# Strassen's algorithm for six of eight column pairs of a second matrix product, and what is moved to make room for it

## The chip, the cores and the metric

The kernel runs on one core of a Trainium2 chip. The time is device microseconds (us) of one execution. Three executions of the kernel before took 1072.84, 1072.2 and 1070.15 us; the median is 1072.2 us. TensorE (PE in the profile) multiplies matrices and writes to PSUM, a memory of eight banks of 512 f32 columns. VectorE (DVE), ScalarE (ACT) and GpSimd (POOL) do the elementwise work, and SyncE (SP) only issues transfers (DMA).

## The reference

Eight batches, eight heads of dimension 64 (512 columns in all), 576 tokens, 32 landmarks, 2048 hidden columns.

```python
def _attn_ref(q, k, v):            # per batch and head
    q_lm, k_lm = mean of q, k over 18 neighbouring tokens      # 32 landmarks
    A, Bm, C = softmax(q k_lm'), softmax(q_lm k_lm'), softmax(q_lm k')
    Z = Bm.T / (norm1(Bm) * norminf(Bm) + 1e-06)
    for _ in range(6):
        Z = 2 * Z - Z @ Bm @ Z
    return A @ Z @ C @ v

def _moe_ref(x, w_ch1, w_ch2):
    mixed = real(fft(fft(x, axis=1), axis=2))
    u = x + mixed
    un = (u - mean(u)) / sqrt(var(u) + 1e-06)
    return u + relu(un @ w_ch1) @ w_ch2
```

## The kernel before

**Numbers.** Products that must be exact to f32 are made of f16 halves: a value is split into `hi` and `lo`, and `mm3` issues three matmuls, hi·hi, hi·lo and lo·hi. The weights come as 64-bit floats, which VectorE rebuilds to f32 by bit operations (`weights`, in 32 pieces of 512 columns: 16 of the first matrix, 16 of the second). Only when all pieces of a matrix are there is its largest magnitude known, hence its scale `wsc`, and only then are its pieces split into halves (`halve`).

**Attention** runs batch by batch in generators. `tokens` loads q, k and v, makes the landmark means `lm`, the scores of all tokens and their softmax, transposes the softmax on TensorE (`AT`), and makes the Fourier sums `CS`. `landmarks` makes the 32 by 32 matrix `Bm`, C and C·v, runs six steps of the pseudo-inverse with E (128x128, block diagonal) against `RE` (32 columns of the power of E and 64 columns of the product with C·v), and then the small matrices `Wt`, `Wx` and `WC`. `mix` turns all of it into the rows `u` in tiles of 128 tokens (4.5 tiles a batch, 36 in all; it makes two tiles of u, normalises both in `norm`, splits them and has SP transpose them by DMA into `unT`).

**Feed-forward** (`mlp`) takes two tiles at a time: 18 chunks of 256 tokens. In a chunk, pair i (of eight) of the hidden blocks is made by `first` matmuls: 24 of 128x256 into a bank `h`. ScalarE applies relu and makes the high half, VectorE makes the low half. `second` multiplies pair i into two banks `acc` (one for each tile), 12 matmuls of 128x512. It comes LAG = 2 pairs behind the first product. After pair 7, VectorE adds `acc` to u, and SP writes it out.

**Order.** A small planner with its own clock (`run`) emits the program: attention first, weights second, feed-forward last. A generator yields until its inputs should be there by the planner's estimates (`till`, with MARGIN = 1.5 us on top), and whoever is ready is emitted. TensorE runs exactly in this order; for the other engines the compiler's scheduler sets the order. So feed-forward matmuls stand between the steps of attention. PSUM is given out as four banks `at` for attention, two for `h` and two for `acc`.

Nearly every VectorE, ScalarE and GpSimd instruction has the line of one helper (L121), and every matmul L197 (a transpose on TensorE L202), so groups are told apart by the names of their tiles.

Of the kernel before, what the change touches and what calls it, by code (L numbers as in the profile page):

```python
# [17 lines left out]
P = 128  # L18
# [8 lines left out]
BIG, MID, ROW, UB, HB, NT, PSH = 8, 7, 6, 7, 4, 3, 2  # L27
# [98 lines left out]
class Kernel:  # L126
    def __init__(self, ctx, tc, NB, q, k, v, w1, w2, t1, t1t, t2, diag, mask, out):
# [6 lines left out]
        self.ps_at, self.ps_h, self.ps_o = psum("ps_at", 8 - PSH - TCH), psum("ps_h", PSH), psum("ps_o", 1)  # L134
        self.loads = {}
        self.now, self.there, self.read, self.used = 0.0, {}, {}, []
# [10 lines left out]
        self.whole = [self.cp.tile([P, NF + 1, 512], F32, name=f"w{w}") for w in range(2)]  # L147
# [22 lines left out]
    def psum(self):  # L170
        t = self.ps_at.tile([P, 512], F32, name="at")
        self.used.append(t.name)
        return t
# [14 lines left out]
    def till(self, *aps, banks=0, more=0.0):  # L188

        last = len(self.used) + banks - (8 - PSH - TCH)  # L190
        free = [self.read.get(n, 0.0) for n in self.used[max(0, last - banks) : max(0, last)]]
        return max(0.0, max([0.0] + free + [self.there.get(a.name, 0.0) for a in aps]) + (MARGIN + more if len(self.unT) > 3 else M0) - self.now)
# [40 lines left out]
    def weights(self):  # L233
        nc = self.nc
        V, A = self.V, self.A
        whole = self.whole
        slots = [[t[:, i] for i in range(NF + 1)] for t in whole]
        am = [self.cp.tile([P, NF], F32, name=f"wmax{w}") for w in range(2)]
        hl = [[t.bitcast(F16).rearrange("p (y m) -> p y m", y=2) for t in ss] for ss in slots]
        self.w1s = [t.rearrange("p y (c f) -> p y c f", c=KT) for t in hl[0]]  # L240
        self.w2s = hl[1]
# [18 lines left out]
        def scale(w):  # L260
            a2 = self.small(1, "wm2")
            V.tensor_reduce(a2, am[w], AX.X, ALU.max)
            yield self.till(a2)
            e, r = yield from self.pow2(a2, 1, f"wp{w}")
            es.append(e)
            V.tensor_scalar(sc[:, w : w + 1], r[:, 0:1], (2.0**6, 2.0**14)[w], None, ALU.mult)

        def halve():
            w, f = pieces[sum(self.split_w)]
            self.split(hl[w][f][:, 0], hl[w][f][:, 1], slots[w][f + 1], sc[:, w : w + 1])  # L270
            self.split_w[w] = f + 1

        for i, (w, f) in enumerate(pieces):
            while len(mags) < min(2 * NF, i + 1 + PREP):
                j = len(mags)
                while len(self.wraw) < min(2 * NF, j + 1 + AHEAD):
                    self.raw()
                if self.raw_there[j] > self.now:
# [4 lines left out]
                prepare(j)  # L283
            rv = self.wraw[i].rearrange("p (m x) -> p m x", x=2)
            top, low = rv[:, :, 1], rv[:, :, 0]
            x, dst = mags[i].bitcast(I32), slots[w][f + 1]
# [11 lines left out]
            if es:  # L298
                halve()
# [14 lines left out]
    def raw(self):  # L314


        i = len(self.wraw)
        w, f = divmod(i, NF)
        room = self.whole[1].rearrange("p i m -> p (i m)").bitcast(I32)
        if w == 0:  # L320
            raw = room[:, 1024 * (f % 8) + 512 : 1024 * (f % 8) + 1536]
            src = self.w1.bitcast(I32).rearrange("(c p) f -> p c f", p=P)
            self.nc.sync.dma_start(raw.rearrange("p (c f) -> p c f", c=KT), src[:, :, 256 * f : 256 * f + 256])
        else:
            at = {3: 9, 4: 11, 5: 13, 6: 15, 11: 13, 12: 15}.get(f)
            if at:
                raw = room[:, 512 * at : 512 * at + 1024]
            else:
                raw = self.big().bitcast(I32)[:, 0:1024]
# [6 lines left out]
    def load(self, b):  # L336
# [3 lines left out]
        res = []  # L340
        for g in range(2):
            kf, qf = self.big(), self.big()
            gs = slice(2 * g, 2 * g + 2)
            nc.sync.dma_start(kf[:, 0 : 2 * S].rearrange("p (r t) -> p r t", r=2), self.k[b, :, gs])
            nc.sync.dma_start(qf[:, 0 : 16 * SEG].rearrange("p (r t) -> p r t", r=2), self.q[b, :, gs])
            for t in (kf, qf):
                self.there[t.name] = self.arrival(0.59)
            res.append([kf, qf])
        for g in range(2):
            for i in range(EARLY if b == 0 else 0):  # L350
                self.raw()
            vf = self.big()
            nc.sync.dma_start(vf.rearrange("p (c d) -> p c d", c=5), self.v[b, g].rearrange("(c p) d -> p c d", p=P))
            self.there[vf.name] = self.arrival(0.66)
            res[g].append(vf)
        self.loads[b] = res

    def tokens(self, b, st):
# [9 lines left out]
        qhs = []  # L368
        for g in range(2):
# [7 lines left out]
            qhs.append(self.big().bitcast(F16))  # L377
            A.activation(qhs[g][:, 0:NQ], qf, AF.Abs, accum_out=am[:, g : g + 1])
# [24 lines left out]
        qm = [h[:, 0:2048].rearrange("p (y r t) -> p y r t", y=2, r=2) for h in qhs]  # L403
        qr = [h[:, 2048:2304].rearrange("p (y r t) -> p y r t", y=2, r=2) for h in qhs]
        for g in range(2):
            qs = loads[g][1][:, 0:NQ].rearrange("p (x t) -> p x t", t=2 * SEG)
# [7 lines left out]
        while b == 1 and self.seconds < NF // 2 - HB:  # L414
            yield 0.5
# [5 lines left out]
        for u in range(3):  # L421
            yield self.till(qhs[min(u, 1)])
# [22 lines left out]
        for u in range(3):  # L445
            ae, w = aes[u], 512 if u < 2 else 128
            yield self.till(ae, banks=1)
            AT = (self.mid() if u < 2 else self.row()).bitcast(F16)[:, 0 : 2 * w].rearrange("p (y t) -> p y t", y=2)
            ps = self.psum()
            for j in range(w // 128):  # L450
                tr(ps[:, 128 * j : 128 * j + 128], ae[:, 128 * j : 128 * j + 128], self.ident)
            split(AT[:, 0], AT[:, 1], ps[:, 0:w], 1.0)
# [11 lines left out]
            else:  # L464
                F2 = ae
            Fh = (self.mid() if u < 2 else self.row()).bitcast(F16)[:, 0 : 2 * w].rearrange("p (y t) -> p y t", y=2)
            A.copy(Fh[:, 0], F2)
            self.G.tensor_tensor(Fh[:, 1], F2, Fh[:, 0], ALU.subtract)
            Fs.append(Fh)
        CS = self.big().bitcast(F16).rearrange("p (g y x t) -> p g y x t", g=2, y=2, x=2)  # L470
# [20 lines left out]

    def landmarks(self, b, st):
# [4 lines left out]
        m4g = lambda m: self.mask4.unsqueeze(1).unsqueeze(3).broadcast_to([P, 2, 4, m])  # L497
        wide = lambda src, m: src.unsqueeze(2).broadcast_to([P, 2, 4, m])
        Bd = sm.tile([P, 2, 32], F32, name="Bd")
        RE = sm.tile([P, 2, 96], F32, name="RE", bufs=3)  # L500
# [25 lines left out]
        while b == 1 and self.seconds < NF // 2 - HB:  # L526
            yield 0.5

        for g in range(2):
            kv = loads[g][0][:, 0 : 2 * S].rearrange("p (r t) -> p r t", r=2)  # L530
# [23 lines left out]
        yield self.till(nrm)  # L554

        psn = self.psum()
        mm(psn[:, 0:128], self.ones_bd.rearrange("p a b -> p (a b)"), nrm.rearrange("p g x m -> p (g x m)"))
        cm = self.small(4, "cm")
        V.tensor_reduce(cm, psn[:, 0:128].rearrange("p (x m) -> p x m", m=32), AX.X, ALU.max)
        ci = self.small(2, "ci")  # L560
        cmv = cm.rearrange("p (g x) -> p g x", x=2)
        V.tensor_tensor(ci, cmv[:, :, 0], cmv[:, :, 1], ALU.mult)
        V.tensor_scalar(ci, ci, 1e-6, None, ALU.add)
        V.reciprocal(ci, ci)
        nci = self.small(2, "nci")
        V.tensor_scalar(nci, ci, -1.0, None, ALU.mult)
        Bbd = sm.tile([P, 2, 4, 32], F32, name="Bbd", bufs=1)
        V.tensor_tensor(Bbd, wide(nrm[:, :, 0, :], 32), m4g(32), ALU.mult)
# [381 lines left out]
```

## Time and profile before

| | |
|---|---|
| median of three runs | 1072.2 us |
| the profiled execution | 1069.82 us, span 1068.0 us (1.8 us lie outside the span) |
| TensorE busy | 983.9 us, 92% of the span |
| VectorE, ScalarE, GpSimd busy | 615.7, 351.6, 111.5 us |
| TensorE idle after 300 us | under 6 us |
| mean granted TensorE clock | 0.973 |

In the groups, "idle before" is what the engine stood still just ahead of an instruction. "mean ns of one" of a matmul holds its pipeline; the spacing of matmuls is read from the chain of waits, where a run such as "x24" is given with its length. A granted clock of 1.00 is full speed. The lines themselves stand in the prediction.

### The profile page before, as it was taken

How to read it: one execution, taken by the hardware profiler on the slowest of the kernel's cores; microseconds unless marked ns; L12 is line 12 of the kernel's file. 1: busy time of each engine (PE TensorE's matmuls, PEld its weight loads, DVE VectorE, ACT ScalarE, POOL GpSimd, SP SyncE). 2: the span in 40 equal slices, each digit the busy share in tenths (PEclk: the TensorE clock that was granted, in tenths of full speed). 3: DMA queues.
4: the chain of work that ended last, by engine and by line, in shares of the span. 5: the costliest groups of instructions: out<-in, count | busy, mean ns of one | idle time of the engine just before them, and what ended most of it. 6: DMA issues, size and time to landing. Idle time of an engine off the chain costs nothing.

```text
span 1068.0 us, 19629 instructions
## 1 busy us (share of the span) xinstructions
PE 983.9 (92%) x8062; PEld 684.6 (64%) x8062; DVE 615.7 (58%) x1673; ACT 351.6 (33%) x797; POOL 111.5 (10%) x125
## 2 busy tenths in 40 slices
PE   1554778999999999999999999999999999999998
PEld 0433535667776676666777677677766677766665
DVE  7889888768562566446745674567451654341111
ACT  4566755334231333123322332233311332111110
POOL 0101102021011020110202020202010020110000
PEclk9766989999999999999999999999999999999999
DMA  9824402223011130110402040114011000110000
GB/s 327 310 99 118 135 25 91 70 50 136 24 39 22 51 109 21 20 41 11 159 1 58 3 153 8 45 17 143 27 41 20 21 1 21 21 48 15 9 20 20
DMA packets 71018, 68.16 MB, mean 64 GB/s; under 512 B 41360, under 2 KB 59792, under 8 KB 70800
## 3 DMA queue, kind: packets, MB, share of 16 engines
q1 hardware_dynamic: 70928, 66.91, 20.3%
q8 instruction: 63, 1.03, 0.4%
q14 instruction: 27, 0.22, 0.1%
HBM read 48.02 MB, written 9.44 MB: 54 GB/s over the span
## 4 chain that ended last, share of the span: by engine, by line
PE 86%; DVE 8%; issue 2%; ACT 2%; DMA 1%; POOL 0%; SPq 0%; ACTq 0%; DVEq 0%
PE acc L197 34%; PE h L197 34%; PE at L197 16%; DVE w L121 2%; PE at L202 2%; DVE row L121 2%; DVE mid L121 1%; ACT row L121 1%; DVE lm L121 1%; DMA big<-q_dram 0%; ACT mid L121 0%; DVE asum L121 0%; DVE big L121 0%; DVE u L121 0%; DVE RE L121 0%
## 5 line engine op out<-in xcount | busy, mean ns | idle before, releaser
L197 PE MATMUL h<-unT,w 128*128 128x256 f16 x3456 | 414.0, 274 | 19.9 <-DMA unT<-row 10.4
L197 PE MATMUL acc<-w,h 128*128 128x512 f16 x1680 | 395.2, 380 | 0.0
L197 PEld LDWEIGHTS <-w 128*128 128x128 f16 x3456 | 335.9, 98 | 92.2 <-issue 19.0
L197 PEld LDWEIGHTS <-h 128*128 128x128 f16 x1680 | 161.7, 98 | 160.9 <-issue 4.1
L121 DVE SCALAR_TENSOR_TENSOR h<-h 128x512 f16<-128x512 f32 x140 | 96.4, 688 | 246.6 <-ACT h L121 246.1
L121 ACT ACTIVATE h<-h 128x512 f16<-128x512 f32 x140 | 83.4, 596 | 359.5 <-PE h L197 359.0
L121 POOL TENSOR_TENSOR r<-ve,mhalf 128x2 f32<-128x2 f32 (+1 forms) x20 | 13.7, 683 | 445.9 <-DVE ve L121 445.9
L197 PEld LDWEIGHTS <-mid 128*128 128x128 f16 x432 | 39.8, 103 | 17.8 <-issue 7.4
L121 POOL TENSOR_TENSOR row<-row 128x512 f16<-128x512 f32 (+1 forms) x44 | 46.6, 1073 | 44.1 <-ACT row L121 44.1
L197 PEld LDWEIGHTS <-big 128*128 128x128 f16 (+1 forms) x768 | 40.6, 104 | 13.0 <-issue 2.4
L121 DVE SCALAR_TENSOR_TENSOR row<-at,scw,row 128x262 f32<-128x262 f32 (+1 forms) x48 | 21.4, 486 | 44.2 <-ACT row L121 31.5
L121 ACT CAST row<-row 128x512 f16<-128x512 f32 (+1 forms) x44 | 23.5, 559 | 70.7 <-DVE row L121 69.9
L121 DVE TENSOR_REDUCE lm<-big 128x32 f32<-128x576 f32 (+1 forms) x48 | 43.8, 943 | 2.7 <-DMA big<-k_dram 2.3
L121 POOL TENSOR_TENSOR mid<-mid,asum 128x512 f32<-128x512 f32 x14 | 14.8, 1055 | 291.7 <-DVE asum L121 291.7
L121 ACT ACTIVATE row<-w 128x512 f32<-128x512 f32 x54 | 33.8, 640 | 21.9 <-DVE w L121 11.4
L121 DVE SCALAR_TENSOR_TENSOR u<-at,scw,row 128x128 f32<-128x128 f32 (+3 forms) x120 | 38.9, 388 | 0.0
L121 POOL TENSOR_TENSOR mid<-mid 128x256 f32<-128x256 f32 (+1 forms) x32 | 31.6, 993 | 65.9 <-DVE mid L121 53.6
L197 PE MATMUL at<-RE,E 128*128 128x96 f32 (+1 forms) x192 | 30.1, 282 | 9.0 <-DVE RE L121 9.0
L197 PEld LDWEIGHTS at<-RE,E 128*128 128x128 f32 x192 | 27.9, 200 | 15.1 <-DVE RE L121 6.6
L197 PE MATMUL at<-mid,big 128*128 128x262 f16 (+1 forms) x288 | 34.1, 290 | 0.0
L121 DVE SCALAR_TENSOR_TENSOR u<-acc,wsc,u 128x512 f32<-128x512 f32 x36 | 26.8, 746 | 12.0 <-PE acc L197 11.7
L121 ACT ACTIVATE w<-w,wsc 128x512 f16<-128x512 f32 x32 | 23.0, 718 | 18.4 <-DVE w L121 12.9
(165 smaller groups left out, 968.5 us busy)
## 6 DMA issues: line engine op xcount, KB each, us to landing
w<-w_dram SPq DMA_DIRECT2D x22, 512.0 KB, 8.8
big<-v_dram SPq DMA_DIRECT2D x16, 640.0 KB, 8.5
big<-q_dram SPq DMA_DIRECT2D x16, 584.0 KB, 5.4
big<-k_dram SPq DMA_DIRECT2D x16, 576.0 KB, 4.3
out_dram<-u SPq DMA_DIRECT2D x36, 256.0 KB, 2.0
big<-w_dram SPq DMA_DIRECT2D x10, 512.0 KB, 7.9
unT<-row SPq DMA_TRANSPOSE x72, 2.4
t<-t_dram SPq DMA_DIRECT2D x1, 1048.0 KB, 10.0
```

The source lines that it names most:

```text
L121: return call(out, *args, **kw)
L197: self.nc.tensor.matmul(out, a, b, start=start, stop=stop, skip_group_check=True)
L202: self.nc.tensor.transpose(out, a, ident)
```

## The change

It has five parts.

1. **Second product.** For pairs 0 to 5 the 2x2 blocks (two tiles of 128 tokens by two hidden blocks, times two hidden blocks by two halves of 256 output columns) are multiplied by Strassen's algorithm in the form with seven products: 7 x 3 matmuls of 128x256 instead of 12 of 128x512. Pairs 6 and 7 stay as they were. The seven sums live in four banks, and after pair 7 they are put together by two ScalarE copies and eight VectorE instructions.
2. **Its left operand.** After relu (ScalarE, to f32 `hf`), VectorE makes four sums or differences of 128 columns, ScalarE makes the high halves of all seven blocks (896 columns), GpSimd the low halves. There is one `hf` buffer until the weights are split, then two; three buffers `h`.
3. **Its right operand.** `halve2` scales the pair (ScalarE, 1024 columns), VectorE makes four differences of 256 columns, ScalarE the high halves (256 and three times 512), VectorE the low halves of 256 and 512, GpSimd those of 512 twice. The raw pieces of the weights now go through a ring of five places, and the first chunk holds at most three pairs `h` before `second` has to begin.
4. **Attention.** It keeps two banks as soon as the second product has begun. The pseudo-inverse is a generator of its own (`inverse`), which carries 64 columns instead of 96, ends in one more product G of 128 columns, and runs beside C·v. The softmax of batches 2 to 7 is transposed by DMA (six more DMA transposes a batch) instead of nine TensorE transposes. v is loaded later, into five instead of eight `big` buffers, and v of batch 0 lies where the last first-matrix weights will lie.
5. **Start of a batch.** A batch may begin as soon as the batch ahead has its `WC`, not its last `mix`.

```diff
-BIG, MID, ROW, UB, HB, NT, PSH = 8, 7, 6, 7, 4, 3, 2
+BIG, MID, ROW, UB, HB, NT, PSH, PSO = 5, 7, 6, 6, 3, 2, 2, 4
+NS = 6
+W2AT = 3 * NS + 4
...
-        self.ps_at, self.ps_h, self.ps_o = psum("ps_at", 8 - PSH - TCH), psum("ps_h", PSH), psum("ps_o", 1)
+        self.ps_at, self.ps_h, self.ps_o = psum("ps_at", 8 - PSH - PSO), psum("ps_h", PSH), psum("ps_o", 1)
...
+        def halve2():
...
+                A.activation(src, src, AF.Copy, scale=sc[:, 1:2])
+                B11, B12, B21, B22 = (src[:, 256 * x : 256 * x + 256] for x in range(4))
+                T13, T24 = self.row(512), self.row(512)
+                (T1, T3), (T2, T4) = ((r[:, 0:256], r[:, 256:512]) for r in (T13, T24))
+                for out, a, b in ((T1, B12, B11), (T3, B22, B12), (T2, B22, T1), (T4, B21, T2)):
+                    V.tensor_tensor(out, a, b, ALU.subtract)
+                flat = t.rearrange("p y x d -> p y (x d)")
+                for a, b, x, eng in ((0, 256, B11, V), (256, 768, src[:, 512:1024], V), (768, 1280, T13, self.G), (1280, 1792, T24, self.G)):
+                    A.copy(flat[:, 0, a:b], x)
+                    eng.tensor_tensor(flat[:, 1, a:b], x, flat[:, 0, a:b], ALU.subtract)
...
+            if b >= 2:
+                for y in range(2):
+                    nc.sync.dma_start_transpose(AT[:, y].rearrange("p (c t) -> p c t", t=P), hl[:, y])
...
+    def inverse(self, st, nrm, nci):
...
+        for it in range(6):
+            yield self.till(E, EP, banks=1, more=NM)
+            c0, c1 = (0 if it < 5 else 32), (64 if it > 0 else 32)
+            ps = self.psum()
+            for g in range(2):
+                mm(ps[:, 64 * g + c0 : 64 * g + c1], flat(E, g), EP[:, g, c0:c1])
...
+        for g in range(2):
+            mm(ps[:, 128 * g : 128 * g + 128], flat(Pbd, g), flat(Bbd, g))
...
+        seven = ((0, 0, 4), (2, 1, 0), (6, 2, 1), (3, 6, 2), (4, 3, 7), (5, 5, 5), (1, 4, 6))
...
-            for t in range(TCH):
-                for x in range(2):
-                    f = 2 * i + x
-                    mm3(acc[t], lambda y: h[:, y, x, P * t : P * t + P], lambda y: self.w2s[f][:, y, :],
-                        start=(f == 0), stop=(f == NF - 1))
+            if i < NS:
+                hv = h.rearrange("p (y x t) -> p y x t", y=2, x=7)
+                for a, b, o in seven:
+                    mm3(acc[o // 2][:, 256 * (o % 2) : 256 * (o % 2) + 256], lambda y: hv[:, y, a], lambda y: self.w2s[i][:, y, b],
+                        start=(i == 0 and o in (0, 2, 4, 7)), stop=(i == NF // 2 - 1))
                     yield 0.0
...
+            if i == NF // 2 - 1:
+                us = self.utiles[TCH * ch : TCH * ch + 2]
...
+                V.tensor_tensor(us[0], us[0], r0, ALU.add)
+                V.tensor_tensor(us[1], us[1], r1, ALU.add)
...
+                while len(late) >= HB:
+                    yield from second(*late.pop(0))
+                h = self.wk.tile([P, 14 * P], F16, name="h", bufs=HB)
+                if i < NS:
+                    f = self.hf[i % 2 if self.split_w[1] == NF else 0]
+                    A11, A21, A12, A22, S1, S2, S4 = (f[:, x] for x in range(7))
+                    A.activation(f[:, 0:4].rearrange("p x t -> p (x t)"), ps, AF.Relu)
+                    V.tensor_tensor(S1, A21, A22, ALU.add)
+                    V.tensor_tensor(A21, A11, A21, ALU.subtract)
+                    V.tensor_tensor(S2, S1, A11, ALU.subtract)
+                    V.tensor_tensor(S4, A12, S2, ALU.subtract)
+                    f, hv = f.rearrange("p x t -> p (x t)"), [h[:, 896 * y : 896 * y + 896] for y in range(2)]
+                    A.copy(hv[0], f)
+                    self.G.tensor_tensor(hv[1], f, hv[0], ALU.subtract)
```

Where instructions now stand shows in three places. The first is VectorE once the second weight matrix has its scale: `wsc` is the scale, `w_74` the second matrix, `row` work space, `Bd` and `bs` belong to batch 1's attention. Before:

```order
L121 RECIPROCAL wp_r<-wp_e 128x1
L121 TENSOR_SCALAR wsc<-wp_e 128x1
L121 TENSOR_SCALAR wsc<-wp_r 128x1
L121 TENSOR_SCALAR Bd<-at 128x64
L121 TENSOR_REDUCE bmx<-Bd 128x2
L121 TENSOR_TENSOR Bd<-Bd,bmx 128x64
L121 SCALAR_TENSOR_TENSOR w_74<-w_74,wsc 128x512
L121 TENSOR_REDUCE bs<-Bd 128x2
```

After, on the same engine at the same place:

```order
L125 TENSOR_SCALAR wsc<-wp_r 128x1
L125 TENSOR_TENSOR row<-w_74 128x256 x2
L125 TENSOR_TENSOR row<-w_74,row 128x256
L125 TENSOR_TENSOR row<-w_74 128x256
L125 TENSOR_TENSOR row<-w_74,row 128x256
L125 TENSOR_TENSOR w_74<-w_74 128x256
L125 TENSOR_TENSOR w_74<-w_74 128x512
L125 TENSOR_TENSOR row<-w_74 128x256
```

One split of 512 columns for each block, with attention between, has become six instructions for each pair, most of them with both inputs in SBUF, and batch 1's attention stands behind the first pairs.

The second place is GpSimd in the same stretch: `r` belongs to the normalisation of batch 0, `mid` and `asum` to batch 1's softmax. Before:

```order
L121 TENSOR_TENSOR r_923<-ve,mhalf 128x2
L121 TENSOR_TENSOR row<-row 128x512 x2
L121 TENSOR_TENSOR mid<-mid,asum 128x512 x2
L121 TENSOR_TENSOR row<-row,asum 128x128
L121 TENSOR_TENSOR mid<-mid 128x256
```

After:

```order
L125 TENSOR_TENSOR r_926<-ve,mhalf 128x2
L125 TENSOR_TENSOR row<-row 128x512 x2
L125 TENSOR_TENSOR h<-hf,h 128x896 x3
L125 TENSOR_TENSOR w_74<-row,w_74 128x512 x7
L125 TENSOR_TENSOR h<-hf,h 128x896
L125 TENSOR_TENSOR w_74<-row,w_74 128x512 x3
L125 TENSOR_TENSOR h<-hf,h 128x896
L125 TENSOR_TENSOR w_74<-row,w_74 128x512
L125 TENSOR_TENSOR h<-hf,h 128x896
L125 TENSOR_TENSOR w_74<-row,w_74 128x512
L125 TENSOR_TENSOR mid<-mid,asum 128x512 x2
```

Where GpSimd had nothing to do between batch 0 and batch 1, six low halves of `h` and twelve of the weights now stand.

The third place is TensorE at the beginning of chunk 6, whose second tile is the first of batch 3 (`Wx` against `mid` is the last matmul of that tile in `mix`). Before, the last such matmul lies three pairs back, and the chunk follows on ordinary pairs:

```order
L197 MATMUL acc_4768<-w_74,h 128x512
L197 LDWEIGHTS h
L197 MATMUL acc_4769<-w_74,h 128x512
L197 LDWEIGHTS w_73
L197 MATMUL h<-unT,w_73 128x256
```

After, the whole way from that matmul to the first of chunk 6, with repeated rows left out:

```order
L209 MATMUL at<-Wx,mid 128x8x32
...
L209 MATMUL acc_5216<-w_74,h 128x256
...
L209 MATMUL acc_5215<-w_74,h 128x512
...
L209 MATMUL at<-mid,big 128x262
...
L209 MATMUL acc_5215<-w_74,h 128x512
L209 MATMUL at<-lm,qbd 64x32 x4
L209 LDWEIGHTS w_73
L209 MATMUL h<-unT,w_73 128x256
```

Between the two stand 21 matmuls of 128x256 and 12 of 128x512 of the second product, 12 of 128x262 of `mix`, and the first four of batch 4. The same sequence, without the last four, stands ahead of chunk 15 (the first tiles of batch 7).

More of the change, by code (lines that the diff above doesn't have):

```diff
@@ L170, in psum @@
     def psum(self):
-        t = self.ps_at.tile([P, 512], F32, name="at")
+        if not self.second_begun and len(self.used) % (8 - PSH) >= 8 - PSH - PSO:
+            t = self.ps_o.tile([P, 512], F32, name=f"acc{len(self.used) % (8 - PSH) - (8 - PSH - PSO)}")
+        else:
+            t = self.ps_at.tile([P, 512], F32, name="at")
+            self.used_at.append(t.name)
         self.used.append(t.name)
@@ L188, in till @@
     def till(self, *aps, banks=0, more=0.0):
-        last = len(self.used) + banks - (8 - PSH - TCH)
-        free = [self.read.get(n, 0.0) for n in self.used[max(0, last - banks) : max(0, last)]]
+        used, n = (self.used_at, 8 - PSH - PSO) if self.second_begun else (self.used, 8 - PSH)
+        last = len(used) + banks - n
+        free = [self.read.get(n, 0.0) for n in used[max(0, last - banks) : max(0, last)]]
         return max(0.0, max([0.0] + free + [self.there.get(a.name, 0.0) for a in aps]) + (MARGIN + more if len(self.unT) > 3 else M0) - self.now)
@@ L283, in weights @@
                 prepare(j)
+            while i >= 10 and not self.v0_used:
+                yield 0.3
             rv = self.wraw[i].rearrange("p (m x) -> p m x", x=2)
             top, low = rv[:, :, 1], rv[:, :, 0]
-            x, dst = mags[i].bitcast(I32), slots[w][f + 1]
+            x, dst = mags[i].bitcast(I32), f32[w][f]
             V.tensor_scalar(x, x, 3, None, ALU.logical_shift_left)
@@ L351, in load @@
                 self.raw()
[L352 to L356, printed above, removed]
+            self.nc.sync.dma_start(tiles[g].rearrange("p (c d) -> p c d", c=5), self.v[b, g].rearrange("(c p) d -> p c d", p=P))
+            self.there[tiles[g].name] = self.arrival(0.66)
+        return tiles
     def tokens(self, b, st):
@@ L413, in tokens @@
                 yield self.till(qhs[0], kbd)
-        while b == 1 and self.seconds < NF // 2 - HB:
+        st["split"] = True
+        while b == 1 and self.seconds < NF // 2 - 4:
             yield 0.5
@@ L469, in tokens @@
             Fs.append(Fh)
+        while "v" not in st:
+            yield 0.3
         CS = self.big().bitcast(F16).rearrange("p (g y x t) -> p g y x t", g=2, y=2, x=2)
@@ L553, in landmarks @@
             crs.append(cr)
[L554 to L568, printed above, removed]
-        yield self.till(Bbd, Ces[0])
-        pst = self.psum()
-        for g in range(2):
-            tr(pst[:, 128 * g : 128 * g + 128], Bbd[:, g].rearrange("p a b -> p (a b)"), self.ident)
-        BT = sm.tile([P, 2, P], F32, name="BT", bufs=1)
-        A.copy(BT.rearrange("p g m -> p (g m)"), pst[:, 0:256])
+        if b > 0:
+            while "split" not in st:
+                yield 0.3
+            vs = self.load_v(b, [self.big(), self.big()])
+        else:
+            vs = self.v0
+        st["v"] = True
+        yield self.till(Ces[0])
         ETs = []
@@ L656, in landmarks @@
             for x in range(2):
+                yield self.till(banks=1)
                 ps = self.psum()
@@ L851, in attention @@
         for b in range(self.NB):
-            while self.folded < b - 1 or (b > 0 and sum(self.split_w) < NF):
+            while self.w_done < b - 1 or (b > 0 and sum(self.split_w) < NF):
                 yield 0.5
```

279 lines of the change are left out of this document (181 added, 98 removed).

## Prediction

> **What bounds the kernel now.** I read the page first: the busy line, the slices, the chain.
>
> ```profile
> PE 983.9 (92%) x8062; PEld 684.6 (64%) x8062; DVE 615.7 (58%) x1673; ACT 351.6 (33%) x797; POOL 111.5 (10%) x125
> PE   1554778999999999999999999999999999999998
> DVE  7889888768562566446745674567451654341111
> PE 86%; DVE 8%; issue 2%; ACT 2%; DMA 1%; POOL 0%; SPq 0%; ACTq 0%; DVEq 0%
> ```
>
> TensorE is full from the ninth slice on (27 us each); its 84 us of idle time lie in the first 200 us, where VectorE is the busy one. So matmuls count from there on, and before it what VectorE must do. Next the chain's end and the windows, which price both:
>
> ```profile
> 1040.86 2.59 PE acc L197 x12
> 1043.45 2.62 PE h L197 x24
> ...
> 120.00:140.00 20.00, 13.35 (x99) 9.75 (x99) 19.93 (x35) 15.33 (x34) 0.00 (x0) 0.93 0.34 110
> 140.00:160.00 20.00, 14.80 (x76) 7.36 (x75) 17.02 (x50) 9.29 (x16) 0.00 (x0) 0.90 0.00 1
> 160.00:180.00 20.00, 17.31 (x220) 10.74 (x219) 17.79 (x54) 12.16 (x30) 3.67 (x5) 1.00 0.37 120
> 180.00:200.00 20.00, 18.90 (x149) 13.05 (x148) 15.99 (x39) 6.22 (x15) 3.27 (x4) 1.00 0.22 64
> 700.00:800.00 100.00, 100.00 (x874) 71.26 (x873) 61.31 (x178) 30.48 (x74) 11.59 (x13) 1.00 0.18 57
> ```
>
> A 128x256 matmul costs 2.62 / 24 = 0.109 us, a 128x512 one 2.59 / 12 = 0.216: half the columns is half the time, although each has its weight load. In 120 to 140 us VectorE is busy 19.93 of 20: it rebuilds the weights, and TensorE waits.
>
> **The gain on TensorE.** A Strassen pair costs 21 x 0.109 = 2.29 us instead of 2.59. With 18 chunks of six pairs that is 108 x 0.30 = 32.1 us less. The attention's matmuls:
>
> ```profile
> 172.24 0.61 PE L197 MATMUL at<-BT 128*128 128x128 f32 x4
> 172.68 0.71 PE L202 MATMUL at<-ident,mid 128*128 128x128 f32 x5
> 173.23 0.81 PE L197 MATMUL acc<-w,h 128*128 128x512 f16 x3
> ```
>
> Five transposes take 173.23 - 172.68 = 0.55 us, so nine in each of six batches are 54 x 0.11 = 5.9 less. G is four passes like those of BT (172.68 - 172.24 = 0.44) in eight batches, 3.5 more. Steps with 64 instead of 96 columns I count as equal: they wait for VectorE more than they compute. Gain: 32.1 + 5.9 - 3.5 = 34.5 us.
>
> **The head: the second matrix is prepared later.** The scale of the second matrix is there at 145.6 us, and splits follow at once:
>
> ```profile
> 139.77 0.16 DVE L121 TENSOR_REDUCE wm<-wmax 128x1 f32<-128x16 f32 x1
> 145.46 0.15 DVE L121 TENSOR_SCALAR wsc<-wp_r 128x1 f32<-128x1 f32 x1
> 146.40 0.75 DVE L121 SCALAR_TENSOR_TENSOR w<-w,wsc 128x512 f16<-128x512 f32 x1
> 46.52 0.69 DVE L121 TENSOR_TENSOR mid<-mid,asum 128x512 f32<-128x512 f32 x1
> 47.12 0.28 DVE L121 TENSOR_TENSOR row<-row,asum 128x128 f32<-128x128 f32 x1
> 47.92 0.75 DVE L121 TENSOR_TENSOR mid<-mid 128x256 f32<-128x256 f32 x2
> 267.40 0.42 POOL L121 TENSOR_TENSOR row<-row 128x128 f16<-128x128 f32 x1
> 268.17 1.16 POOL L121 TENSOR_TENSOR mid<-mid 128x512 f16<-128x512 f32 x1 [0.34 <-ACT mid L121]
> L121 ACT CAST row<-row 128x512 f16<-128x512 f32 x36 | 21.1, 617 | 70.7 <-DVE row L121 69.9 <-POOL row L121 0.6
> L121 ACT ACTIVATE big<-big,sc 128x1024 f16<-128x1024 f32 x16 | 18.4, 1148 | 0.0
> L121 DVE SCALAR_TENSOR_TENSOR big<-big,sc 128x1024 f16<-128x1024 f32 x16 | 20.5, 1279 | 1.0 <-ACT big L121 1.0
> ```
>
> From here on the first chunk's pairs 3 to 5 and the six Strassen weight pairs are made together, since only three buffers `h` may wait. Until the sixth weight pair is there, this must run:
> - VectorE with two SBUF inputs: 30 of 128x256 at 0.38 = 11.3; six of 512 at 0.69 = 4.1; twelve of 128x128 for `h` at 0.28 = 3.4; batch 1's q, twice 1.28 and 0.35 = 3.3. Together 22.1 us.
> - GpSimd: twelve of 512 at 1.16 = 13.9; three of 896, which no row shows. By the slope of its two rows, (1.16 - 0.42) / 384 = 1.93 ns a column, one is 1.16 + 384 x 1.93 ns = 1.90 us: 5.7. Together 19.6 us.
> - ScalarE: six scalings at 1.15, eighteen copies of 512 at 0.62, six of 256 at about 0.36, and some 11 us of relu, copies and batch 1's work: 31 us.
>
> Do VectorE and GpSimd overlap? These rows say no:
>
> ```profile
> 93.59 0.74 DVE L121 SCALAR_TENSOR_TENSOR w<-w,wsc 128x512 f16<-128x512 f32 x1
> 96.43 1.72 POOL L121 TENSOR_TENSOR row<-row 128x512 f16<-128x512 f32 x1 [5.94 <-ACT row L121]
> 97.06 1.64 DVE L121 SCALAR_TENSOR_TENSOR w<-w,wsc 128x512 f16<-128x512 f32 x1
> ```
>
> The same VectorE instruction takes 0.74 us alone and 1.64 beside GpSimd, and ends half a microsecond after GpSimd does; GpSimd's took 1.72 instead of 1.16. One works while the other waits. So the stretch lasts 22.1 + 19.6 = 41.7 us rather than ScalarE's 31; I take 41.7, the end that these rows speak for. Its beginning I put at 147.5: up to there VectorE loses seven low halves of `h` (7 x 0.69) and gains twelve sums and two or three small steps, about even, and three GpSimd instructions of 1.90 us now get in its way (bounds 145.5 and 151). The sixth pair is thus there at 189.2 us.
>
> Before, TensorE had done the same work (all of chunk 0's first product, six pairs of its second, the same steps of batch 1) at about 172.8: at 172.7 it still lacks a quarter of pair 4 and pair 5 (3.2 us) but is ahead by one pair of chunk 1 and five transposes (2.6 + 0.6). TensorE itself needs only 6 x 2.29 + 5 x 2.62 = 27 us plus small steps in that stretch, so it waits. Loss: 189.2 - 172.8 = 16.4 us; bounds 4 (145.5 + 31) and 28 (151 + 41.7 + 8 for chains that don't fill).
>
> **Two chunks that begin too early.** A tile's way from `mix` to `unT` shows at chunk 0:
>
> ```profile
> 89.87 2.77 PE L197 MATMUL at<-Wx,mid 128*128 128x256 f16 x12
> 103.08 2.93 PE L197 MATMUL h<-unT,w 128*128 128x256 f16 x12 [10.45 <-DMA unT<-row]
> ```
>
> From 92.64 to 103.08: 10.4 us. At chunks 6 and 15 the order now leaves 21 x 0.109 + 12 x 0.216 + 12 x 0.11 (262 columns) and four small ones between = 6.4 us; before, 25 us stood there. TensorE waits 4.0 us at each, 8 in all (up to 16 when GpSimd's two steps of that way each wait for one of its 1.90).
>
> The Trainium skill, "TensorE: Matmul & The Clock Gate", section "What's actually happening", says that an idle window of about 3.4 us halves the clock until as much busy time has passed. By that rule each of the two waits costs up to another 1.7 us, and the time would be some 3 us more. The row at 103.08 agrees in kind (twelve matmuls in 2.93 us, 0.244 each, after 10.45 us of idle time), but no row shows a wait of 4 us, and I leave it to the upper end.
>
> **What is hidden.** Per pair, VectorE gives up one low half and takes four sums, about even:
>
> ```profile
> L121 DVE SCALAR_TENSOR_TENSOR h<-h 128x512 f16<-128x512 f32 x140 | 96.4, 688 | 246.6 <-ACT h L121 246.1
> L121 ACT ACTIVATE h<-h 128x512 f16<-128x512 f32 x140 | 83.4, 596 | 359.5 <-PE h L197 359.0
> L121 DVE SCALAR_TENSOR_TENSOR u<-acc,wsc,u 128x512 f32<-128x512 f32 x36 | 26.8, 746 | 12.0 <-PE acc L197 11.7
> ```
>
> ScalarE takes 896 columns more (about 1.0 us), GpSimd 1.90. The way of a pair is 0.6 + 4 x 0.28 + 1.0 + 1.9 = 4.6 us; the second product comes two pairs later, 2 x (2.62 + 2.29) = 9.8 us, and hides it with 5 us to spare. Per chunk GpSimd gets 11.4 us more and VectorE six additions at the end (3 us), against 100 us of TensorE in which 61 and 12 are busy (window 700 to 800): neither becomes the bound. The banks `acc` are free again 1.5 us after a chunk's last product (two at 0.75), behind 2.62 us of other matmuls. Six more transposes a batch stand on SP's queue; behind them wait loads that are needed some ten microseconds later. Cover gone, the attention's steps come late.
>
> That is the unknown: two banks instead of four, and VectorE and GpSimd in each other's way, against the planner's margin of 1.5 us. Between 300 and 1000 us TensorE now loses almost nothing (100.00 of 100 in the window). One wait is a rest of 1.90 - 1.5 = 0.4 us at most, two at once 2.3. Ends: 0 and 15 us (about one late step of 2.3 in each of six batches); nearest to the row is a small one, 4. At the end one addition of 512 more, 0.69. A gain in these terms is excluded, since nothing there waits today.
>
> **The sum.** -34.5 + 16.4 + 8 + 4 + 0.7 = -5.4 us, 1062.6 against the span of 1068.0. The profiled execution lies 1.8 us above its span and 2.4 below the median of 1072.2; with both, 1066.8, or 1067.
>
> **The rivals.**
> - *The head costs little* (+4): ScalarE sets the stretch and the two engines overlap better than in those three rows. 1067 - 12 = 1055. For it: VectorE's 22 us need not meet GpSimd each time. Against: the rows.
> - *Gain and loss cancel*: head 20, waits 12, late steps 5: +2.5, about 1075 to 1069. For it: every loss has room upwards, the gain has none.
> - *Slower: GpSimd holds up attention*, one mechanism, place: VectorE's two-input steps of batches 2 to 7 behind the 102 GpSimd instructions of 1.90 us. If two steps a batch meet two of them in a row, 12 x 2.3 = 28 us instead of 4: 1091. It decides from four late steps on (5.4 + 3.2 = 8.6 us above the 4 taken). For it: GpSimd goes from 12 to some 35 busy us in 100. Against: VectorE has 39 of 100 free. The Trainium skill, "SBUF — State Buffer", section "Who interferes with whom", says that a VectorE instruction with two SBUF inputs and a GpSimd one that reads SBUF block each other for the whole instruction, whoever is first; the row of 1.64 us agrees, and by that rule this rival has no softer form.
> - *Slower: the second matrix itself comes late.* Its last four loads now stand behind chunk 0's transposes on SP, and rebuilding waits for them: 6 us on the beginning, 5 on the stretch: 1078. Against: a load lands 8 us after its issue, and four pieces last 13.
> - *The matmuls don't halve*: weight loads of `h` (98 ns each) stop hiding behind 109. At 0.120 us a matmul, 2268 x 0.011 = 25 us: 1092. Against: the 24 in 2.62 us have the same loads.
>
> **How the numbers follow.** What this measurement tells from no change is 0.3%, 3.2 us. Forecast as worked out (1057 to 1069): 0.36. Little head cost: 0.14. Cancel: 0.20. GpSimd holds up attention: 0.13; late matrix: 0.12; matmuls that don't halve: 0.05. Faster 0.50, same 0.20, slower 0.30. The forecast's own range is 1057 to 1069; for 8 in 10 it reaches to 1049 (head nearly free, nothing late) and to 1087 (either slower case, short of its full price).
>
> **What would show it.** Right: `acc` 128x256 as x21 in 2.29 us in the chain; the low half of `h` on GpSimd near 1.9 us; the sixth weight pair near 189 us, TensorE full some 16 us later than before; waits of about 4 us for `unT` at the beginnings of chunks 6 and 15; elsewhere few. Wrong: TensorE with idle time spread over the middle (late steps), or a head that ends before 180 or after 200 us.

## The result: 143 us slower

The changed kernel takes 1215.6 us (median of four, 1214.1 to 1216.7), the kernel before 1072.5 (median of four): a ratio of 1.133, 95% interval 1.131 to 1.136. Forecast were 1067 us and a range up to 1087. The profiled execution has a span of 1214.9 us.

First the page of the changed kernel: busy time, the slices of TensorE and VectorE, and the clock.

```profile
PE 1004.2 (83%) x9012; PEld 792.7 (65%) x9012; DVE 785.9 (65%) x2119; ACT 491.7 (40%) x977; POOL 356.3 (29%) x257
PE   1654176888999799978988798979989899989998
DVE  7888996666677557665676636663678655646532
PEclk9667588898999899989999798998999899999999
```

Before, the TensorE row was 9 from the ninth slice on, up to the last. Now 8s and 7s stand everywhere up to the end, and below them the clock falls to 8 and 7 as well. No slice explains the loss alone. TensorE is busy for 20 us more than before (1004.2 against 983.9) although it has less to do. The windows up to and behind 200 us, first of the kernel before, then of the changed one, and its 120 to 140 us (busy time of PE, PEld, DVE, ACT, POOL, then the clock):

```profile
0.00:200.00 200.00, 121.99 (x998) 82.98 (x999) 172.76 (x438) 115.92 (x262) 21.45 (x27) 0.85 0.47 154
200.00:1068.00 868.00, 861.91 (x7065) 601.61 (x7063) 442.90 (x1236) 235.68 (x536) 90.06 (x98) 1.00 0.15 43
```

```profile
0.00:200.00 200.00, 90.50 (x702) 67.15 (x703) 168.19 (x416) 121.87 (x263) 45.96 (x37) 0.74 0.42 135
200.00:1214.90 1014.90, 913.68 (x8313) 725.55 (x8310) 617.75 (x1704) 369.83 (x714) 310.37 (x220) 0.95 0.16 44
120.00:140.00 20.00, 0.00 (x0) 0.00 (x0) 19.24 (x37) 14.87 (x31) 3.42 (x1) 0.50 0.32 99
```

- Up to 200 us TensorE stands idle for 109.5 us instead of 78.0.
- After 200 us it stands idle for 101.2 us (1014.9 - 913.68) instead of 6.1, and the mean clock is 0.95 instead of 1.00. Half of its busy time in the stretches at half clock, counted over the trace, is 41 us; before, nothing. This half is my estimate of what the lower clock costs.
- Its busy time at full clock (busy time less that half) fell from 965.6 to 941.1 us.

So 31.5 us of idle time and 4 of clock were lost in the head, 95 and 41 behind it, and 24.5 us of work were saved: 147 us, the difference of the spans. The question is who TensorE waits for after 200 us. The waits of that stretch (us in total, times, longest), of the changed kernel:

```profile
PE at L209 <- ACT mid L125: 30.6, 19, 4.2
PE at L214 <- ACT mid L125: 17.6, 8, 3.3
PE at L209 <- DVE big L125: 12.1, 11, 1.6
PE at L209 <- DVE nrm L125: 9.5, 5, 4.2
PE h L209 <- DMA unT<-row: 8.2, 4, 2.4
```

A step `at` waits for a step that writes `mid` or `big`. That looks like missing data, but mostly isn't: what is written there has been read out of a bank `at`, and TensorE waits for the bank. One such place in order of time (start, length, and in brackets the idle time before):

```profile
686.31 0.71 PE L209 MATMUL at<-big,qbd 128*64 128x288 f32 x4 [1.09 <-issue]
687.26 0.71 PE L209 MATMUL at<-big,qbd 128*64 128x288 f32 x4 [0.25 <-DVE u L125]
690.15 1.28 DVE L125 SCALAR_TENSOR_TENSOR big<-big,sc 128x1024 f16<-128x1024 f32 x1
691.35 0.15 DVE L125 TENSOR_SCALAR cb<-cb 128x1 f32<-128x1 f32 x1
691.53 0.50 ACT L125 ACTIVATE mid<-at,cb 128x288 f32<-128x288 f32 x1 [2.07 <-DVE cb L125]
692.17 1.22 PE L209 MATMUL at<-BT 128*128 128x128 f32 x4 [4.21 <-ACT mid L125]
```

The scores of C fill both banks of attention at 687.97. The next matmul in TensorE's order is one of the pseudo-inverse; its input `BT` has long been there, but it needs a bank. The first bank is read out by the exponential on ScalarE at 691.5, which waits for `cb` on VectorE, which stands behind a 1.28 us scaling of q. TensorE waits 4.2 us with feed-forward matmuls queued behind. Of the 96.5 us that it stands idle between 200 and 1210 us, about 62 are of this kind: by the names of the tiles, the releaser only reads a bank and makes no input of the waiting matmul.

The same stretch of waits in the two kernels without Strassen, first with two banks for attention, then with four (the experiments below):

```profile
PE at L209 <- ACT mid L125: 19.5, 18, 3.3
PE at L214 <- ACT mid L125: 14.4, 8, 3.3
PE at L209 <- DVE big L125: 12.1, 10, 1.8
```

```profile
PE at L214 <- ACT mid L125: 5.7, 3, 3.1
PE at L209 <- DVE nrm L125: 1.2, 2, 0.6
```

### The profile page after: what moved, and what is told of

It reads as the page before. It is cut to its first block, busy times and chain, and to the rows that moved or that the text cites. A ratio compares the mean times of both kernels' runs of the same rounds, so it can differ in the third digit from the quotient of the medians.

```text
span 1214.9 us, 22597 instructions
## 1 busy us (share of the span) xinstructions
PE 1004.2 (83%) x9012; PEld 792.7 (65%) x9012; DVE 785.9 (65%) x2119; ACT 491.7 (40%) x977; POOL 356.3 (29%) x257
## 5 line engine op out<-in xcount | busy, mean ns | idle before, releaser
L209 PE MATMUL acc<-w,h 128*128 128x256 f16 (+1 forms) x2700 | 392.3, 298 | 4.7 <-ACT w L125 3.4
L209 PEld LDWEIGHTS <-h 128*128 128x128 f16 x2700 | 267.9, 101 | 81.6 <-issue 14.4
L125 POOL TENSOR_TENSOR h<-hf,h 128x896 f16<-128x896 f32 x57 | 111.1, 1949 | 409.9 <-ACT h L125 358.3
L125 POOL TENSOR_TENSOR h<-w,h 128x896 f16<-128x896 f32 x51 | 98.7, 1935 | 172.6 <-ACT h L125 87.0
L125 DVE TENSOR_TENSOR w<-w 128x128 f32<-128x128 f32 (+1 forms) x216 | 82.2, 398 | 69.1 <-ACT w L125 67.1
L125 DVE TENSOR_TENSOR hf<-hf 128x128 f32<-128x128 f32 x228 | 78.1, 360 | 61.4 <-ACT hf L125 58.4
L125 ACT CAST h<-hf 128x896 f16<-128x896 f32 x57 | 53.4, 937 | 81.6 <-DVE hf L125 74.2
L125 ACT CAST h<-w 128x896 f16<-128x896 f32 x51 | 47.8, 938 | 79.9 <-DVE w L125 68.5
L125 DVE SCALAR_TENSOR_TENSOR h<-h 128x512 f16<-128x512 f32 x36 | 24.8, 690 | 60.2 <-ACT h L125 60.0
L125 ACT ACTIVATE h<-h 128x512 f16<-128x512 f32 x36 | 21.5, 596 | 63.0 <-PE h L209 62.9
L125 POOL TENSOR_TENSOR r<-ve,mhalf 128x2 f32<-128x2 f32 (+1 forms) x20 | 15.2, 759 | 101.6 <-DVE ve L125 101.2
```

Of the source, the lines that this page charges most:

```text
L125: return call(out, *args, **kw)
L209: self.nc.tensor.matmul(out, a, b, start=start, stop=stop, skip_group_check=True)
```

## The experiments

Each stands against the kernel before on the same chip (medians 1071.4 to 1072.2 us). The theory at the start was that two banks make the loss; the first rival, that GpSimd holds VectorE up. Four of them make a square, which carries the argument:

| | attention keeps four banks | two banks |
|---|---|---|
| ordinary second product | 1087.7 | 1162.8 |
| Strassen | 1128.5 (its sums in two banks) | 1215.6 (the changed kernel) |

**Asking again** (`e1_recheck`). All 27 places of this form:

```diff
-            yield self.till(banks=2)
+            yield from self.wait(banks=2)
+    def wait(self, *aps, **kw):
+        yield self.till(*aps, **kw)
+        while self.till(*aps, **kw) > 0.0:
+            yield self.till(*aps, **kw)
```

> The changed kernel, but a generator that resumes asks again whether its inputs and banks are there, and yields again if not (until now it trusted the answer that it got before another generator took a bank). Theory banks: of the 96.5 us that TensorE stands idle after 200 us, 63 wait for a bank, and the 41 us that the halved clock costs there follow those waits; both fall to a quarter, 1216 - 75 = about 1140 us (1115 to 1165). Theory GpSimd lock: the steps are late because VectorE is held up, asking again changes little: 1200 to 1220.

Measured: 1195.7 us, ratio 1.116 (1.113 to 1.118). It fits neither range. Generators that trusted an old answer cost 20 us. The rest of the waits moved to other steps: TensorE still stands idle for 94 us after 200 us, and the clock costs 41 as before. The waits after 200 us now lead so:

```profile
PE at L219 <- ACT mid L125: 21.0, 8, 6.5
PE at L214 <- ACT mid L125: 16.8, 7, 4.4
PE at L214 <- ACT row L125: 13.9, 4, 4.8
```

**Low halves on VectorE** (`e2_low_on_vector`).

```diff
-                    self.G.tensor_tensor(hv[1], f, hv[0], ALU.subtract)
+                    V.tensor_tensor(hv[1], f, hv[0], ALU.subtract)
```

> The changed kernel, with the low halves of the seven Strassen blocks (896 columns) on VectorE instead of GpSimd. Theory GpSimd lock: VectorE loses the 91 us by which its instructions after 200 us are longer than alone, takes 108 x about 1.2 = 130 us of new work off no critical path, and the attention steps are no longer held up for 1.9 us at a time: 1216 - 60 = about 1155 us. Theory banks: the bank waits of TensorE stay, 1200 to 1235.

Measured: 1211.1 us, ratio 1.130 (1.128 to 1.132). With two banks it hardly matters who makes the low halves, and the 60 us of the GpSimd theory are not there: GpSimd is not the first cause. The 4 us are a net figure, since VectorE takes on 108 instructions of 1.10 us for them.

**Without Strassen, four banks** (`e3_plain_four_banks`) **and two** (`e4_plain_two_banks`). PSO is the number of banks of the second product, PSH that of the first. The first kernel has PSO = 2, the second PSO = 4 with two of the four unused:

```diff
-... PSH, PSO = 5, 7, 6, 6, 3, 2, 2, 4
-NS = 6
-W2AT = 3 * NS + 4
+... PSH, PSO = 5, 7, 6, 6, 3, 2, 2, 2
+NS = 0
+W2AT = 22
...
-                r0, r1 = self.row(512), self.row(512)
...
+                for t, u in enumerate(us):
+                    V.scalar_tensor_tensor(u, acc[t], self.inv2, u, ALU.mult, ALU.add)
```

> The changed kernel without Strassen: all eight pairs by the ordinary second product, two banks for its sums, so that attention keeps four; everything else of the change stays (three buffers h, ring of five, transposes by DMA, pseudo-inverse with G, early start of a batch). Theory banks: the middle is full again; against 1072 only the shorter run-ahead of the first chunk costs, some 15 us, less 2 to 5 for the transposes: about 1082 (1070 to 1095). Theory order (the transposes by DMA, the early batch start and the new inverse bring the waits): above 1130.

> As the ordinary second product with four banks, but attention keeps only two banks once the second product has begun, as in the changed kernel. Theory banks: the waits for banks are back without any of Strassen's work: 70 to 110 us above the kernel with four banks, about 1170. Theory GpSimd lock: GpSimd has none of the low halves here, so no more than 15 us above the one with four banks.

Measured: 1087.7 us, ratio 1.015 (1.013 to 1.017), and 1162.8 us, ratio 1.086 (1.083 to 1.088). Two banks less cost 75 us where nothing of Strassen's is in the kernel. With four, TensorE is idle for 12.2 us after 200 us, with two for 58.8. The transposes by DMA, the new pseudo-inverse and the early start of a batch do not bring the waits.

**The kernel before with two banks** (`e5_before_two_banks`).

```diff
-self.ps_at, self.ps_h, self.ps_o = psum("ps_at", 8 - PSH - TCH), ...
+self.ps_at, self.ps_h, self.ps_o = psum("ps_at", 2), ...
...
+        wf = self.row(256)
+        A.copy(wf[:, 0:128], ps[:, 0:128])
+        A.copy(wf[:, 128:256], pst[:, 0:128])
```

> The kernel before, but attention keeps two banks instead of four once the second product has begun (two banks lie unused); the two small results of the pseudo-inverse are copied out of their banks first, without which two banks block each other. Theory banks: the price is that of the pair without Strassen (1163 - 1088 = 75 us) or a little less, since nothing else of the change is in it: about 1135 us (1115 to 1155). Theory order (two banks cost only together with the generator of its own for the pseudo-inverse): below 1095.

Measured: 1137.5 us, ratio 1.061 (1.058 to 1.065). The price of two banks, with the two small copies that they need, is 66 us by itself. TensorE's idle time after 200 us goes from 6.1 to 46.2 us (937.4 - 891.23):

```profile
200.00:1137.40 937.40, 891.23 (x7139) 609.41 (x7136) 462.19 (x1256) 243.58 (x554) 89.95 (x98) 0.99 0.14 42
```

**Strassen with four banks** (`e6_strassen_four_banks`). The seven sums go to two banks:

```diff
-... PSH, PSO = 5, 7, 6, 6, 3, 2, 2, 4
+... PSH, PSO = 5, 7, 6, 6, 3, 2, 2, 2
...
-seven = ((0, 0, 4), (2, 1, 0), (6, 2, 1), (3, 6, 2), (4, 3, 7), (5, 5, 5), (1, 4, 6))
+seven = ((0, 0, 0), (2, 1, 0), (6, 2, 1), (3, 6, 2), (4, 3, 3), (5, 5, 1), (1, 4, 2))
...
```

> The changed kernel with all of Strassen's work (six weight pairs, sums, low halves on GpSimd, 21 matmuls of 128x256 a pair, the final additions), but its seven sums are added up in two banks instead of four, so that attention keeps four; the output is therefore not the reference's. Theory banks: the kernel without Strassen and four banks took 1088; 32 us less matmuls, 12 us more head, 8 for the two early chunks: about 1078 (1062 to 1092). Theory elementwise (the sums and GpSimd's work delay attention, as the 53 us between 1163 and 1216 could say): 1120 to 1145.

Measured: 1128.5 us, ratio 1.053 (1.051 to 1.055). My theory of banks alone falls here: with plenty of banks Strassen still loses 41 us against the ordinary product. Its busy time at full clock is 933.3 us against 960.9 there, so the matmuls do save 27.5; what surrounds them costs 68, 14 of them in the head. The waits after 200 us are mostly of another kind, for results of VectorE's small steps; of 46 us of idle time between 200 and 1120 us, some 20 are still for a bank (most of the first of these lines):

```profile
PE at L209 <- DVE big L125: 10.6, 8, 2.6
PE at L209 <- DVE EP L125: 9.3, 5, 2.7
PE at L209 <- DVE nrm L125: 7.7, 2, 3.8
```

**Two banks, without the left operand's work** (`e7_strassen_light`).

```diff
-                    mm3(... lambda y: hv[:, y, a], ...
+                    mm3(... lambda y: hv[:, y, a % 4], ...
...
-                    A.activation(f[:, 0:4].rearrange("p x t -> p (x t)"), ps, AF.Relu)
-                    V.tensor_tensor(S1, A21, A22, ALU.add)
...
-                    self.G.tensor_tensor(hv[1], f, hv[0], ALU.subtract)
+                    hv = [h[:, 896 * y : 896 * y + 512] for y in range(2)]
+                    A.activation(hv[0], ps, AF.Relu)
+                    V.scalar_tensor_tensor(hv[1], ps, 0.0, hv[0], ALU.max, ALU.subtract)
```

> The changed kernel with two attention banks and all its matmuls, but the left operand is made as before (ScalarE relu and high half of 512 columns, VectorE low half), the four sums, the 896-column copies and GpSimd's low halves of h are left out, and three of the seven blocks are read from others; the output is therefore not the reference's. Theory elementwise: this work makes the 53 us: about 1150 (1130 to 1165). Theory chain (two banks make attention a chain that ends each batch, and Strassen's shorter matmuls leave less to fill it): about 1200 (1185 to 1215).

Measured: 1170.3 us, ratio 1.093 (1.090 to 1.095); 45 us less than the changed kernel, five above the range of the elementwise theory. With two banks too, the elementwise work makes most of Strassen's 53 us (1215.6 - 1162.8).

**Three banks** (`e8_one_h_bank`). PSH = 1 instead of 2, on top of asking again.

> The changed kernel with one bank for the first product instead of two, so that attention keeps three beside Strassen's four, and with generators that ask again before they take a bank. Theory banks: most of the price of two banks goes; TensorE has Strassen's 2.3 us to wait for the relu of one bank: about 1115 us (1090 to 1140). Theory elementwise: the waits are for late steps and not for banks, and one bank less for the first product adds to them: 1180 to 1210.

Measured: 1134.8 us, ratio 1.059 (1.057 to 1.061). One bank more for attention, taken from the first product, gives 61 us (1195.7 - 1134.8). It is the best whole Strassen kernel of these runs, and still 63 us behind the kernel before.

**What of Strassen's work holds attention up**, at four banks (against 1128.5). `e9_four_banks_low_on_vector` is the edit of e2 on e6; `e10_four_banks_no_sums` is this, four times:

```diff
-                    V.tensor_tensor(S1, A21, A22, ALU.add)
+                    if ch < 2: V.tensor_tensor(S1, A21, A22, ALU.add)
```

> The kernel with all of Strassen's work and four attention banks (its sums added up in two banks, so the output is not the reference's; 1128.5 us), with the low halves of 896 columns on VectorE instead of GpSimd. What is open: why Strassen costs 41 us against the ordinary product (1087.7) when banks are plenty. Theory GpSimd lock: the 109 us by which VectorE's instructions after 200 us are longer than alone go, about 1100 us (1088 to 1112). Theory VectorE load (four sums, six additions and the weights make VectorE's queue longer, whoever does the low halves): 1125 to 1150.

> The same kernel with Strassen, four banks and GpSimd's low halves, but from the third chunk on the four sums on VectorE are left out (the copies and low halves of 896 columns stay; the output is not the reference's). Theory VectorE load: 96 x 4 instructions of 0.28 to 0.4 us less on the queue that attention waits for, about 1100 us (1088 to 1112). Theory GpSimd lock: the two-input instructions of attention are still held up for 1.9 us: 1115 to 1130.

Measured: 1112.1 us, ratio 1.038 (1.037 to 1.040), and 1098.0 us, ratio 1.024 (1.022 to 1.026). The first lies at the upper edge of the range of the GpSimd theory, the second within that of VectorE's load. Both theories hold a part: 16 us go with GpSimd's low halves (net of the same work on VectorE), 30 with the sums. The two overlap, since a sum that GpSimd blocks is counted in both; how they divide stays open. A kernel with four banks and neither was not run. The groups of the changed kernel (busy us, mean ns of one), and behind them the same three VectorE groups of e2, where GpSimd makes no low halves of `h` (half of the sums stand under `w`, where the second `hf` buffer lies):

```profile
L125 POOL TENSOR_TENSOR h<-hf,h 128x896 f16<-128x896 f32 x57 | 111.1, 1949 | 409.9 <-ACT h L125 358.3 <-issue 23.0 <-PE h L209 10.0
L125 DVE TENSOR_TENSOR hf<-hf 128x128 f32<-128x128 f32 x228 | 78.1, 360 | 61.4 <-ACT hf L125 58.4
L125 DVE TENSOR_TENSOR w<-w 128x128 f32<-128x128 f32 x204 | 73.9, 380 | 69.1 <-ACT w L125 67.1
L125 DVE TENSOR_TENSOR u<-u,row 128x512 f32<-128x512 f32 x36 | 32.6, 917 | 0.2
```

```profile
L125 DVE TENSOR_TENSOR hf<-hf 128x128 f32<-128x128 f32 x228 | 75.4, 348 | 39.6 <-ACT hf L125 37.2
L125 DVE TENSOR_TENSOR w<-w 128x128 f32<-128x128 f32 x204 | 60.4, 314 | 30.0 <-ACT w L125 27.8
L125 DVE TENSOR_TENSOR u<-u,row 128x512 f32<-128x512 f32 x36 | 24.8, 698 | 0.2
```

A VectorE instruction of 128 columns with two inputs in SBUF took 0.28 us in the kernel before, one of 512 columns 0.69. In the changed kernel they take 0.36 to 0.38 and 0.92 on the mean. Without GpSimd's low halves the long ones are back at 0.70, the sums only at 0.31 to 0.35, so a part of what lengthens the sums is not the low halves. Over all VectorE instructions after 200 us, the time beyond what the fastest tenth of each group takes is 95 us in the changed kernel and 51 in e2; at four banks it is 109 (e6) and 57 (e9). About half of it goes with the low halves.

**The head** (`e11_plain_run_ahead`), on the kernel of e3:

```diff
-... HB, NT, PSH, PSO = 5, 7, 6, 6, 3, 2, 2, 2
+... HB, NT, PSH, PSO = 5, 7, 6, 6, 4, 2, 2, 2
...
-                while len(late) >= HB:
-                    yield from second(*late.pop(0))
-                h = self.wk.tile([P, 14 * P], F16, name="h", bufs=HB)
+                if ch > 0 or i >= NF // 2 - HB:
+                    h = self.wk.tile([P, 8 * P], F16, name="h", bufs=HB)
+                else:
+                    h = self.mid().bitcast(F16)[:, 0 : 8 * P]
...
-                while len(late) >= LAG:
+                while len(late) >= LAG and (ch > 0 or self.split_w[1] >= 2 * late[0][1] + 2):
```

> The changed kernel without Strassen and with four attention banks (1087.7 us), and the first chunk's run-ahead as before: four buffers h of the size that the ordinary product needs, the first four pairs of the first chunk in work space, and no second product before its weights are there. Theory run-ahead: the head's extra 13 us (91 + 19 against 78 + 18 us of idle time and lost clock up to 200 us) come from the three buffers: 1070 to 1076. Theory ring: they come from the ring of five raw pieces and the later loads, then 1083 to 1088.

Measured: 1077.0 us, ratio 1.0045 (1.003 to 1.006). That is 1 us above the range of the run-ahead theory and far below that of the other: 11 of the 16 us by which e3 lies above the kernel before are the run-ahead of chunk 0, and where the other 5 come from stays open. With three buffers TensorE does nothing from 120 to 140 us; with eight places it works again (first e3, then e11):

```profile
120.00:140.00 20.00, 0.37 (x1) 0.08 (x1) 18.62 (x37) 13.52 (x31) 0.00 (x0) 0.50 0.31 105
```

```profile
120.00:140.00 20.00, 11.32 (x85) 7.31 (x86) 18.80 (x34) 16.76 (x36) 0.00 (x0) 1.00 0.30 105
```

**A part that gains by itself** (`e12_before_dma_transposes`), in the kernel before:

```diff
+            if b < 2:
...
+            else:
+                yield self.till(ae)
+                hl = self.row(2 * w, F16).rearrange("p (y t) -> p y t", y=2)
+                A.copy(hl[:, 0], ae)
+                self.G.tensor_tensor(hl[:, 1], ae, hl[:, 0], ALU.subtract)
+                for y in range(2):
+                    nc.sync.dma_start_transpose(AT[:, y].rearrange("p (c t) -> p c t", t=P), hl[:, y])
...
```

> The kernel before with one part of the change alone: batches 2 to 7 transpose their softmax by DMA (copy on ScalarE, low half on GpSimd, six more DMA transposes a batch) instead of by nine TensorE transposes. By the term of the prediction 54 x 0.11 = 5.9 us less: 1065.5 us (1063 to 1069). Rival: the transposes' landing is later than the planner's 4 us and a wait takes back what TensorE saves: 1070 to 1076.

Measured: 1066.2 us, ratio 0.995 (0.994 to 0.996). This version beats both kernels.

## Why the prediction was wrong, point by point

**The gain on TensorE was right in its prices.** A Strassen pair takes 2.29 us in the chain of the changed kernel, as worked out:

```profile
1155.32 2.62 PE h L209 x24
1157.93 2.29 PE acc L209 x21
```

The transposes are worth 6.0 us by themselves (e12), forecast 5.9. At four banks Strassen's matmuls save 27.5 us; no run explains the 4.6 that are missing to the 32.1. The rival that matmuls don't halve is out.

**The head was right in its moment and wrong in its price.** The sixth weight pair is there at 184.7 us; 189.2 was forecast. The stretch lasts 38.1 us from the first of its VectorE sums (146.52); forecast were 41.7 from 147.5.

```profile
182.91 1.20 POOL L125 TENSOR_TENSOR w<-row,w 128x512 f16<-128x512 f32 x1
183.02 1.64 DVE L125 TENSOR_TENSOR w<-w 128x512 f16<-128x512 f32 x1
142.27 0.37 PE L214 MATMUL at<-ident,wm 128*1 128x128 f32 x1 [27.47 <-DVE wm L125]
```

The VectorE row of 1.64 us beside GpSimd's, where the kernel before had 0.69 for 512 columns, bears out that the two exclude each other. But I compared only the two ends. The row at 142.27 shows that TensorE stood still for 27.5 us before, because only three pairs fit ahead: idle time and lost clock up to 200 us are 36 us more than before, not 16.4. Of these the kernel of e3 already has 14 (mostly the run-ahead, e11), two banks bring it to 24 (e4), and Strassen's work with four banks to 28 (e6).

**The chunks that begin too early were right**: 8 us forecast, and at chunks 6 and 15 TensorE waits 1.13 + 2.38 and 2.41 + 2.32 = 8.2 us.

```profile
525.56 0.27 PE L209 MATMUL h<-unT,w 128*128 128x256 f16 x1 [1.13 <-DMA unT<-row]
528.21 2.08 PE L209 MATMUL h<-unT,w 128*128 128x256 f16 x9 [2.38 <-DMA unT<-row]
1080.60 0.28 PE L209 MATMUL h<-unT,w 128*128 128x256 f16 x1 [2.41 <-DMA unT<-row]
1083.20 2.10 PE L209 MATMUL h<-unT,w 128*128 128x256 f16 x9 [2.32 <-DMA unT<-row]
```

Behind them the clock is at half from 526.7 to 533.5 and from 1083.1 to 1086.5 us. Half of the busy time there is 4.3 us; the prediction had some 3 and left it to the upper end.

**The step that failed is "That is the unknown: two banks instead of four".** I took 4 us for late steps from it and from GpSimd, with ends of 0 and 15, and priced no clock there. Measured are 95 us of idle time and 41 of clock behind the head, of which chunks 6 and 15 are 8 and 4. It is spread over the middle, as the prediction's own sign of being wrong has it. The square prices the two banks at 75 us without Strassen's work and 87 with it (1215.6 - 1128.5). I priced one GpSimd instruction against the planner's margin, and took "loses almost nothing" between 300 and 1000 us as a sign of slack. It was slack made of banks: with two banks, TensorE in the kernel before stands idle for 46.2 us after 200 us (e5). What counts is how long a bank is held: the scores of C hold both for 4.2 us (687.97 to 692.1), and the order puts the pseudo-inverse right behind. The planner's own figures, an estimate and no measurement, say the same: once the fourth pair of tiles is under way, the program of before takes no bank ahead of the planned time at which it is free, that of after takes 44, by 49 us in sum. That sum was to be had before the run.

**"What is hidden" failed second.** I set four sums against one low half as "about even" (1.12 against 0.69 us; the sums took 0.36 to 0.38 each instead of 0.28). VectorE's busy time after 200 us rose by 175 us; its steps for attention stand in that queue. At four banks what surrounds the matmuls turns a gain of 27.5 us into a loss of 41; without the sums the loss is 10 (1098.0 against 1087.7).

**The rivals.** GpSimd holding up attention was there. Moving its low halves to VectorE gains 16 us at four banks (e9) and 4 at two (e2), net of 1.10 us more on VectorE for each; the rival gave 28, and what the blocking costs without that extra work no run shows. The Trainium skill, "SBUF — State Buffer", section "Who interferes with whom", has the two engines lock each other out; the row at 183.02 agrees (1.64 us instead of 0.69). The late second matrix did not happen: rebuilding ends at 140.9 us, `wsc` is there at 145.3. No rival named the banks, so nothing in the range stood for them.

## What to carry to other kernels

A bank taken from a chain of small steps can cost the time for which a step holds its bank; count the steps and read the holding times (end of the matmuls to end of the last reader) before calling a pool large enough. A full TensorE row shows that the waits are covered, not that the cover can be given away. Saved matmul time has to be set against the queue of the engine that prepares the operands, when that engine also carries the latency chain.

## What the runs showed of the hardware

The clock falls after much shorter pauses than I had assumed. Windows of the changed kernel on the trace's own grid of 3.41 us (length, busy time of each engine, clock):

```profile
676.88:680.30 3.42, 1.75 (x14) 1.27 (x13) 1.84 (x13) 1.45 (x5) 0.33 (x1) 1.00 0.00 0
680.30:683.71 3.41, 3.41 (x18) 2.45 (x17) 2.81 (x9) 2.53 (x5) 0.00 (x0) 0.50 0.00 0
683.71:687.12 3.41, 2.21 (x18) 1.30 (x15) 2.52 (x10) 0.94 (x1) 0.02 (x1) 1.00 0.00 0
687.12:690.54 3.42, 0.71 (x4) 0.23 (x4) 2.90 (x11) 1.46 (x2) 2.59 (x2) 1.00 0.02 5
690.54:693.95 3.41, 1.78 (x8) 1.53 (x9) 3.25 (x12) 2.12 (x6) 0.74 (x1) 0.50 0.77 225
693.95:697.36 3.41, 3.41 (x18) 2.41 (x17) 1.54 (x3) 0.00 (x0) 1.53 (x2) 0.50 0.46 159
697.36:700.78 3.42, 3.42 (x33) 3.06 (x32) 0.36 (x2) 0.60 (x1) 0.00 (x0) 1.00 0.00 0
```

A window with TensorE idle for 1.67 us (3.42 - 1.75) is followed by one at half clock; one with 1.20 us idle (683.71) is not. After 200 us in this trace every window at full clock with 2.0 us idle or more is followed by half clock, none with under 1.6; in between both occur (1.67 us fell, 1.95 did not). The clock comes back only behind a window that was full or nearly so (at most 0.13 us idle). So 1.7 us of idle time in one window can cost another 1.7 us, half of the window behind it, and this is 41 of the 136 us. The Trainium skill, "TensorE: Matmul & The Clock Gate", section "What's actually happening", speaks of an idle window of about 3.4 us; the grid agrees, but the windows here need to be idle for only about half.
